# Decode attention with an MLP branch on one core: wo products, MLP pieces, value products and the last unit moved to other places in the order of work

## The chip, the core and the metric

The kernel runs on one NeuronCore of a Trainium2 chip. Its engines are TensorE (PE; PEld is its weight load), VectorE (DVE), ScalarE (ACT), GpSimd (POOL) and SyncE (SP), which here only issues transfers. Each engine works through its own instructions in order; semaphores order them against each other. The metric is the device time of one launch in microseconds (us). The time before is the median of three runs.

## What is computed

One decode step for 4 sequences: x is 4 x 640; layer normalisation gives xn. The result is x + A(xn) + B(xn).

```
A: q = xn @ wq                              # 32 heads of 128
   scores = q . k_cache * 128 ** -0.5       # 4 x 32 x 4096, no mask
   p = softmax(scores)
   o = p @ v_cache;  A = o @ wo             # wo: 4096 x 640
B: z = gelu(xn @ w_in)                      # tanh form; two halves of 864
   z2 = layernorm(z[864:])
   g = w_sp[0, 0] * z2 + b_sp[0]
   B = (z[:864] * g) @ w_out                # w_out: 864 x 640
```

All inputs are bf16. The K and V caches are 134 MB each; the profile counts 282.24 MB read from HBM in all. There is one query per head, so every element of K and V is used once.

## The kernel before

**Units and steps.** The work of attention is cut into 16 units: unit u = 4 hg + b is sequence b with the 8 heads of group hg (4 groups). A unit's K is 128 partitions x 256 rows of 128 numbers, 8.4 MB, and so is its V. A unit has 4 steps of 64 rows each; step n belongs to unit n // 4 and i = n % 4 is its place in it.

**A step.** VectorE multiplies a run of K by the broadcast q in place (`product`, L481) and adds its halves (`fold_half`, L487). TensorE adds the remaining 64 columns by 8 products with the identity (`sums`, L496). VectorE finishes the row sums (`row_sums`, L509), one step late, behind the next step's product. At the first step of a unit the unit before is finished: `head_max` (L518 to L525), `exps` on ScalarE (L531), `by_head` on VectorE (L542), which lays the weights out by head in `p_m` (two places, taken in turn).

**Value products.** `weighted` (L566) multiplies V by `p_m`, 64 products on TensorE; `take` (L578) copies the sum out on ScalarE. `turns` says behind which step of the next unit they stand: step 2 of it for units 0 to 11, step 3 for units 12 and 13. Unit 14's stand at the very end, behind the last exponentials and the denominators. At the first step of the unit after, `picked` gathers the rows of each head (L597; L644 in the last group).

**End of a group.** After the fourth unit of a group, `group_den` and `group_turn` give the group's denominators and the normalised, transposed heads (L607, L609, L617 on VectorE, at step 0 of a unit), and `group_proj` (L627) multiplies them with the group's wo rows, 16 products into `out_ps`, behind step 1's sums.

**Places and loads.** K lies in a ring of 7 places of one step each (`k_ring`); V has one place (`v_all`), which also holds wq, w_in and the end of w_out at the start. The rest of w_out lies in `p_m`. Odd units have ring places 0 to 3, even ones 3 to 6, and the last two units are placed apart; wo of a group lies in place 6, which the even units use too. All loads stand in one list, in order: the V of a unit, then the K of the unit two on, and so forth, with wo behind the K at the end of a group; the list's end interleaves halves of K with V, and unit 15's V goes to the ring in pieces. `pump` at the end of each step issues the loads of this list on SyncE until one needs a place that is still in use (`busy`); a place is given free where the program order has its last reader, and SyncE then waits for that reader by semaphore. So K of unit 6 and K of unit 10 come behind `group_proj`, and each V load behind the `weighted` of the unit before.

**The MLP.** `gmlp` (L347 to L454) is written behind the sums of step 1 as one block: 70 products `zT` (L355), the GELU (L362 to L375), sums for the norm (L380), the norm's factors on one partition (L389 to L416), their broadcast (L425), and 14 products into `out_ps` (L446). V's place is given free behind it.

**Order.** TensorE, VectorE, ScalarE and SyncE keep the order in which the program is written (`manual_schedule`); no planner moves anything.

Of the kernel before, what the change touches and what calls it, by code (L numbers as in the profile page):

```python
# [17 lines left out]
def kernel(  # L18
# [16 lines left out]
    Bsz, Sq, D = A_x.shape  # L35
# [16 lines left out]
    HG = H // HT  # L52
# [294 lines left out]
    def gmlp():  # L347
        zz, gw, gt, gz = (gm[n] for n in ("zz", "gw", "gt", "gz"))
        zT = ps_pv.tile([P, 2, NFC, Bsz], FP32, tag="pv", name="zT")
        for t in range(2):  # L350
            f1 = t * Fh + NFF * P
            w_t = w_in_sb[:, :, t * Fh : f1].rearrange("p c (f k) -> p c k f", k=NFF)
            for k in range(NFC):
                for c in range(DC):
                    nc.tensor.matmul(  # L355
                        out=zT[: P if k < NFF else FT, t, k, :],
                        lhsT=w_t[:, c, k, :] if k < NFF else w_in_sb[:, c, f1 : f1 + FT],
                        rhs=xnT[:, c, 0:Bsz],
                        start=(c == 0),
                        stop=(c == DC - 1),  # L360
                    )
        nc.vector.tensor_copy(out=zz[:, :, 0:NFF, :], in_=zT[:, :, 0:NFF, :])  # L362
        nc.vector.tensor_copy(out=zz[:FT, :, NFF, :], in_=zT[:FT, :, NFF, :])
        nc.vector.tensor_tensor(out=gw[:], in0=zz[:], in1=zz[:], op=ALU.mult)
        nc.vector.tensor_scalar(
            out=gw[:], in0=gw[:], scalar1=0.044715, scalar2=1.0, op0=ALU.mult, op1=ALU.add
        )
        nc.vector.tensor_tensor(out=gw[:], in0=gw[:], in1=zz[:], op=ALU.mult)
        nc.scalar.activation(
            out=gt[:], in_=gw[:], func=ACT.Tanh, scale=math.sqrt(2.0 / math.pi)  # L370
        )
        nc.vector.tensor_scalar(
            out=gt[:], in0=gt[:], scalar1=1.0, scalar2=0.5, op0=ALU.add, op1=ALU.mult
        )
        nc.vector.tensor_tensor(out=gz[:, 0:2], in0=zz[:], in1=gt[:], op=ALU.mult)  # L375
        sq = gz[:, 2, :, :]
        nc.vector.tensor_tensor(out=sq, in0=gz[:, 1, :, :], in1=gz[:, 1, :, :], op=ALU.mult)

        s_ps = ps_m.tile([1, 2, NFC, Bsz], FP32, tag="m", name="ln_ps")
        nc.tensor.matmul(  # L380
            out=s_ps[:], lhsT=ones_sq[:, 0:1], rhs=gz[:, 1:3], start=True, stop=True
        )
        st, ac = gm["st"], gm["ac"]
        mean_t = st[:, 0:Bsz]
        ex2_t = st[:, Bsz : 2 * Bsz]
        var_t = st[:, 2 * Bsz : 3 * Bsz]
        rst_t = st[:, 3 * Bsz : 4 * Bsz]
        tmp_t = st[:, 4 * Bsz : 5 * Bsz]
        nc.vector.tensor_reduce(  # L389
            out=st[:, 0 : 2 * Bsz].rearrange("o (s b) -> o s b", s=2),  # L390
            in_=s_ps[:].rearrange("o s k b -> o s b k"),
            axis=AX.X,
            op=ALU.add,
        )
        nc.vector.tensor_scalar(
            out=st[:, 0 : 2 * Bsz],
            in0=st[:, 0 : 2 * Bsz],
            scalar1=1.0 / float(Fh),
            scalar2=None,
            op0=ALU.mult,  # L400
        )
        nc.vector.tensor_tensor(out=tmp_t, in0=mean_t, in1=mean_t, op=ALU.mult)
        nc.vector.tensor_tensor(out=var_t, in0=ex2_t, in1=tmp_t, op=ALU.subtract)
        nc.scalar.activation(
            out=rst_t, in_=var_t, func=ACT.Sqrt, bias=eps_tile[:1], scale=1.0
        )
        wsp_t = work.tile([1, 1], FP32, name="wsp_t")
        nc.vector.tensor_copy(out=wsp_t[:], in_=wsp_bf[:])
        bsp_t = work.tile([1, 1], FP32, name="bsp_t")
        nc.vector.tensor_copy(out=bsp_t[:], in_=bsp_bf[:])  # L410
        nc.vector.reciprocal(out=rst_t, in_=rst_t)
        nc.vector.tensor_scalar(
            out=ac[:, 0:Bsz], in0=rst_t, scalar1=wsp_t[:, 0:1], scalar2=None, op0=ALU.mult
        )
        nc.vector.tensor_tensor(out=tmp_t, in0=ac[:, 0:Bsz], in1=mean_t, op=ALU.mult)
        nc.vector.tensor_scalar(  # L416
            out=ac[:, Bsz : 2 * Bsz],
            in0=tmp_t,
            scalar1=-1.0,
            scalar2=bsp_t[:, 0:1],  # L420
            op0=ALU.mult,
            op1=ALU.add,
        )
        ac_ps = ps_m.tile([P, 2 * Bsz], FP32, tag="m", name="ac_ps")
        nc.tensor.matmul(  # L425
            out=ac_ps[:], lhsT=ones_sq[0:1, :], rhs=ac[:], start=True, stop=True
        )
        ac_sb = work.tile([P, 2 * Bsz], FP32, name="ac_sb")
        nc.scalar.copy(out=ac_sb[:], in_=ac_ps[:])
        nc.vector.tensor_tensor(  # L430
            out=sq,
            in0=gz[:, 1, :, :],
            in1=ac_sb[:, None, 0:Bsz].to_broadcast([P, NFC, Bsz]),
            op=ALU.mult,
        )
        nc.vector.tensor_tensor(
            out=sq,
            in0=sq,
            in1=ac_sb[:, None, Bsz : 2 * Bsz].to_broadcast([P, NFC, Bsz]),
            op=ALU.add,  # L440
        )
        nc.vector.tensor_tensor(out=gm["yT"][:], in0=gz[:, 0, :, :], in1=sq, op=ALU.mult)
        for k in range(NFC):
            w = P if k < NFF else FT
            for half in range(2):
                nc.tensor.matmul(  # L446
                    out=out_sum(half),
                    lhsT=gm["yT"][:w, k, :],
                    rhs=(w_out_sb[:, k] if k < NFF else w_end_sb[:FT])[
                        :, half * NOH : (half + 1) * NOH  # L450
                    ],
                    start=False,
                    stop=False,
                )  # L454

    qbcs, scores, pvs = {}, {}, {}
    sums_ps, maxes, p_c = {}, {}, {}
# [21 lines left out]
    def product(n):  # L479
        u, r, t = step(n)  # L480
        nc.vector.tensor_tensor(  # L481
            out=t, in0=t, in1=qbcs[u][:, None, :].to_broadcast([P, HC, Dh]), op=ALU.mult
        )

    def fold_half(n):
        u, r, t = step(n)
        nc.vector.tensor_tensor(  # L487
            out=t[:, :, 0:HD2], in0=t[:, :, 0:HD2], in1=t[:, :, HD2:Dh], op=ALU.add
        )
# [134 lines left out]
    def group_proj(hg):  # L624
        for n, o in enumerate(gr.pop(hg)):
            for half in range(2):
                nc.tensor.matmul(  # L627
                    out=out_sum(half),
                    lhsT=o,
                    rhs=wo_sb[:, n, half * NOH : (half + 1) * NOH],  # L630
                    start=False,
                    stop=(hg == HG - 1 and n == HT - 1),
                )
        busy.remove(WO_AT)
# [18 lines left out]
        (pick_last if u // Bsz == HG - 1 else pick_unit)(u)  # L653


    turns = {NK * (u + 1) + 2: u for u in range(NU - 4)}
    turns[NK * (NU - 3) + 3] = NU - 4
    turns[NK * (NU - 2) + 3] = NU - 3

    E = mybir.EngineType  # L660
    with tc.manual_schedule(engines={E.PE, E.DVE, E.Activation, E.SP}):
        stage_q(0)
        waiting, closed = None, None
        for n in range(NK * NU):
            u, i = divmod(n, NK)
            product(n)
            if n:
                row_sums(n - 1)
            if i == 0 and u:
                head_max(u - 1)  # L670
                if waiting is not None:
                    picked(waiting)
                    if waiting % Bsz == Bsz - 1 and waiting // Bsz < HG - 1:
                        closed = waiting // Bsz
                    waiting = None
            fold_half(n)
            if i == 0 and u:
                exps(u - 1)
                by_head(u - 1)
            sums(n)  # L680
            if closed is not None:
                if i == 0:
                    group_turn(closed)
                else:
                    group_proj(closed)
                    closed = None
            if i == 0 and u + 1 < NU:
                stage_q(u + 1)
            if n == 1:
                gmlp()  # L690
                busy.remove(V)
            if n in turns:
                w = waiting = turns[n]
                if w % Bsz == Bsz - 1:
                    group_den(w // Bsz)
                weighted(w, v_runs)
                take(w)
                busy.remove(V)
            pump()
        row_sums(NK * NU - 1)  # L700
        head_max(NU - 1)
        exps(NU - 1)
# [8 lines left out]
        )  # L711
        rden = small.tile([P, NQ, PAR, Bsz], FP32, name="rden_all")
        nc.vector.reciprocal(out=rden[:], in_=den[:])
        weighted(NU - 2, v_runs)
        take(NU - 2)
        picked(NU - 2)
        u, b = NU - 1, Bsz - 1
        weighted(u, v_ends[0])
# [50 lines left out]
```

## Time and profile before

| what | us |
|---|---|
| median of three runs (679.65 to 680.65) | 680.4 |
| the profiled execution's own time | 679.59 |
| its span | 677.8 |
| VectorE busy | 522.5 |
| TensorE busy | 303.5 |
| L481 products busy (64) | 282.7 |
| L487 folds busy (64) | 145.9 |
| VectorE waiting for K | 98.1 |

The transfers moved 282.54 MB, 417 GB/s over the span; the queue of SyncE took 97.3% of the time of the 16 DMA engines. The mean granted clock of TensorE was 0.682 of its full speed.

How to read what follows: a group line has the source line, the engine, the operation, output and inputs with sizes, then the busy time, the mean of one in ns, and the idle time before it with what ended it. The page's slices divide the span by 40, some 16.9 us each. The chain of waits has start, length and what ended last; a DMA in it is the time from its issue to its landing. Times inside the execution are counted from the start of the span.

### The profile page before, as it was taken

Reading aid. Unit: us, or ns where it says so; the run is one execution under the profiler, and the core shown is the slowest. Engines: PE = TensorE matmul, PEld = TensorE weight load, DVE = VectorE, ACT = ScalarE, POOL = GpSimd, SP = SyncE. Lnnn points to the kernel's source line nnn. Section 1 sums busy time; section 2 is a strip of 40 time slices with the busy share of each in tenths; the row PEclk is TensorE's granted clock in tenths of the full one; section 3 lists DMA queues with packets and bytes.
Section 4 is the critical chain, followed back from the end, with each engine's and each line's share of the span. In section 5 each row is a group of like instructions: output and inputs, shape, how many; then the busy total and the mean of one; then the engine's idle time right before and its main releaser. Section 6 shows DMA issues by size and latency. Waiting matters only on the chain.

```text
span 677.8 us, 4614 instructions
## 1 busy us (share of the span) xinstructions
PE 303.5 (45%) x1999; PEld 128.0 (19%) x1999; DVE 522.5 (77%) x325; ACT 29.6 (4%) x73; POOL 2.7 (0%) x12
## 2 busy tenths in 40 slices
PE   0353472614546271452624546045462624636347
PEld 0131121211213020120211213012120211212114
DVE  2549989959696992968969696596969969997950
ACT  0010000000000000000000000000000000000000
POOL 1000000000000000000000000000000000000000
PEclk9755666767857676586766868558675766766678
DMA  9999999999999979999999989999999999999995
GB/s 374 438 438 433 434 419 418 430 433 433 434 433 379 465 321 433 430 433 429 426 426 437 403 375 372 433 433 434 433 434 433 433 437 430 401 451 428 436 405 204
DMA packets 8128, 282.54 MB, mean 417 GB/s; under 512 B 832, under 2 KB 1964, under 8 KB 3116
## 3 DMA queue, kind: packets, MB, share of 16 engines
q1 hardware_dynamic: 8088, 282.24, 97.3%
q8 instruction: 15, 0.25, 0.1%
q14 instruction: 5, 0.04, 0.0%
q10 hardware_dynamic: 20, 0.01, 0.0%
HBM read 282.24 MB, written 0.01 MB: 416 GB/s over the span
## 4 chain that ended last, share of the span: by engine, by line
DMA 54%; DVE 31%; PE 13%; issue 1%; ACT 1%; SPq 0%; DVEq 0%; ACTq 0%
DMA k_ring<-in_A_k_cache_dram 50%; DVE k_ring L481 16%; DVE k_ring L487 8%; PE s_ps L496 8%; DMA v_all<-in_A_v_cache_dram 5%; PE pv L566 2%; DVE s_sb L509 2%; DVE p_m L542 2%; DVE m L518 1%; PE out_ps L627 1%; PE zT L355 1%; PE o_last L722 0%; DVE mt L520 0%; DVE mt L523 0%; DVE nm L525 0%
## 5 line engine op out<-in xcount | busy, mean ns | idle before, releaser
L481 DVE TENSOR_TENSOR k_ring<-k_ring,qbc 128x8192 bf16<-128x8192 bf16 x64 | 282.7, 4417 | 98.1 <-DMA k_ring<-in_A_k_cache_dram 98.1
L496 PE MATMUL s_ps<-k_ring,ident 128*128 128x512 bf16 x512 | 199.9, 561 | 339.6 <-DVE k_ring L487 339.3
L496 PEld LDWEIGHTS <-ident 128*128 128x128 bf16 x512 | 65.9, 130 | 453.5 <-issue 379.5
L487 DVE TENSOR_TENSOR k_ring<-k_ring 128x4096 bf16<-128x4096 bf16 x64 | 145.9, 2280 | 0.0
L566 PE MATMUL pv<-v_all,p_m 128*32 128x512 bf16 x960 | 62.8, 421 | 2.4 <-DMA v_all<-in_A_v_cache_dram 2.4
L509 DVE TENSOR_REDUCE s_sb<-s_ps 128x64 f32<-128x512 f32 x64 | 43.6, 682 | 3.4 <-PE s_ps L496 3.4
L542 DVE TENSOR_TENSOR p_m<-p_c,own 128x2048 bf16<-128x2048 bf16 x16 | 36.6, 2286 | 5.2 <-ACT p_c L531 5.2
L566 PEld LDWEIGHTS <-p_m 128*32 128x32 bf16 x992 | 26.7, 105 | 41.4 <-issue 21.6
L578 ACT COPY o_rows<-pv 128x512 f32<-128x512 f32 x16 | 9.4, 586 | 314.2 <-PE pv L566 314.2
L531 ACT ACTIVATE p_c<-s_sb,nm 128x256 bf16<-128x256 f32 x16 | 8.1, 508 | 205.3 <-DVE nm L525 205.3
L597 PEld LDWEIGHTS o_ps<-o_rows,pick 128*128 128x128 f32 x96 | 12.6, 191 | 1.7
L597 PE MATMUL o_ps<-o_rows,pick 128*128 128x128 f32 x96 | 12.6, 275 | 0.0
L278 DVE TENSOR_SCALAR q_rows<-q_ps 128x512 bf16<-128x512 f32 x2 | 1.4, 692 | 13.7 <-PE q_ps L270 13.7
L730 DVE TENSOR_TENSOR o_n_last<-o_last,rden_all 128x32 bf16<-128x32 f32 x1 | 0.2, 193 | 14.3 <-PE o_last L722 14.3
L270 PE MATMUL q_ps<-v_all,xnT 128*32 128x512 bf16 x40 | 4.5, 630 | 10.4 <-DMA v_all<-in_A_wq_dram 10.4
L471 ACT CAST qbc<-qbc_ps 128x128 bf16<-128x128 f32 x16 | 4.3, 266 | 104.6 <-PE qbc_ps L463 104.6
L518 DVE TENSOR_REDUCE m<-s_sb 128x1 f32<-128x256 f32 x16 | 6.7, 420 | 0.6
L463 PE MATMUL qbc_ps<-q_rows,of_row 128*128 128x128 bf16 x32 | 6.4, 291 | 0.6 <-DVE q_rows L278 0.6
L463 PEld LDWEIGHTS <-of_row 128*128 128x128 bf16 x32 | 4.4, 139 | 8.5 <-issue 8.2
L362 DVE COPY zz<-zT 128x48 f32<-128x48 f32 x1 | 0.2, 207 | 7.2 <-PE zT L355 7.2
L644 PE MATMUL o_last<-hot,o_rows 128*128 128x8 f32 x32 | 4.2, 259 | 2.9 <-ACT o_rows L578 2.9
L644 PEld LDWEIGHTS o_last<-hot,o_rows 128*128 128x128 f32 x32 | 3.9, 191 | 4.9 <-ACT o_rows L578 4.9
(87 smaller groups left out, 71.3 us busy)
## 6 DMA issues: line engine op xcount, KB each, us to landing
k_ring<-in_A_k_cache_dram SPq DMA_DIRECT2D x6, 4096.0 KB, 20.6
v_all<-in_A_wq_dram SPq DMA_DIRECT2D x1, 5120.0 KB, 15.3
k_ring<-in_A_v_cache_dram SPq DMA_DIRECT2D x1, 4096.0 KB, 32.8
k_ring<-in_A_wo_dram SPq DMA_DIRECT2D x3, 1280.0 KB, 7.4
v_all<-in_B_w_in_dram SPq DMA_DIRECT2D x1, 2160.0 KB, 29.2
k_ring<-in_A_v_cache_dram SPq DMA_DIRECT2D x1, 2048.0 KB, 35.0
k_ring<-in_A_v_cache_dram SPq DMA_DIRECT2D x1, 1024.0 KB
k_ring<-in_A_v_cache_dram SPq DMA_DIRECT2D x2, 512.0 KB
```

The costliest lines, as they stand in the source:

```text
L463: nc.tensor.matmul(out=qb_ps[:], lhsT=of_row[:, e, b].rearrange("p k f l -> p (k f l)"), rhs=q_rows[e][:, hg, :], start=(e == 0), stop=(e ...
L481: nc.vector.tensor_tensor(out=t, in0=t, in1=qbcs[u][:, None, :].to_broadcast([P, HC, Dh]), op=ALU.mult)
L487: nc.vector.tensor_tensor(out=t[:, :, 0:HD2], in0=t[:, :, 0:HD2], in1=t[:, :, HD2:Dh], op=ALU.add)
L496: nc.tensor.matmul(out=s[:], lhsT=ident[:], rhs=t[:, :, g * RW : (g + 1) * RW], start=(g == 0), stop=(g == m - 1),)
L509: nc.vector.tensor_reduce(out=scores[u][:, r * HC : (r + 1) * HC], in_=sums_ps.pop(n)[:], axis=AX.X, op=ALU.add,)
L518: nc.vector.tensor_reduce(out=m1[:], in_=scores[u][:], axis=AX.X, op=ALU.max)
L531: nc.scalar.activation(out=p_c[u][:], in_=scores.pop(u)[:], func=ACT.Exp, bias=maxes.pop(u)[:], scale=1.0, accum_out=row_den[hg % NACC][:, ...
L542: nc.vector.tensor_tensor(out=p_m[:, u % 2], in0=p_c.pop(u)[:].rearrange("p (g c) -> p g c", c=CB)[:, :, :, None].to_broadcast([P, NG, CB, HT]
L566: nc.tensor.matmul(out=pvs[u][cg * QD : (cg + 1) * QD, :], lhsT=p_m[:, u % 2, g0 + n].rearrange("p c h -> p (c h)"), rhs=v_at[:, n * CB : ...
L578: nc.scalar.copy(out=o[:].rearrange("p c d -> p (c d)"), in_=pvs.pop(u)[:])
L597: nc.tensor.matmul(out=gr[hg][:], lhsT=pick[:, c, Bsz - 1 - b : P + Bsz - 1 - b], rhs=o[:, c, :], start=(b == 0 and c == 0), stop=(b == Bs ...
L644: nc.tensor.matmul(out=o_last[0][:, :, :, u % Bsz], lhsT=o[:, c, :], rhs=hot[:, c, :].rearrange("p (e k) -> p k e", e=PAR), start=(c == 0) ...
```

## The change

Four moves; no operation is added or left out.

1. `gmlp` becomes a generator of six pieces. The `zT` products stand behind step 0's sums and the next q broadcast. Behind step 1's product comes the GELU up to the tanh; behind step 1's fold come the rest of the GELU with the sums for the norm, and the norm's first factors; then step 1's sums. Behind step 2's product come the other factors and their broadcast, behind its fold the last piece with the 14 output products; then step 2's sums. V's place is given free behind step 2.
2. `turns` of units 0 to 11 say step 1, not step 2, of the next unit.
3. `group_turn` and `group_proj` stand together behind step 0's sums and the q broadcast of the unit after a group; before, the broadcast stood behind `group_turn`, and `group_proj` stood behind step 1's sums.
4. `weighted` and `take` of unit 14 stand ahead of the last `row_sums`, `head_max`, `exps` and `by_head`, directly behind the last sums.

```diff
@@ gmlp @@
                         stop=(c == DC - 1),
                     )
+        yield
         nc.vector.tensor_copy(out=zz[:, :, 0:NFF, :], in_=zT[:, :, 0:NFF, :])
...
             out=gt[:], in_=gw[:], func=ACT.Tanh, scale=math.sqrt(2.0 / math.pi)
         )
+        yield
...
             out=s_ps[:], lhsT=ones_sq[:, 0:1], rhs=gz[:, 1:3], start=True, stop=True
         )
+        yield
...
         nc.vector.tensor_copy(out=bsp_t[:], in_=bsp_bf[:])
+        yield
         nc.vector.reciprocal(out=rst_t, in_=rst_t)
...
         nc.scalar.copy(out=ac_sb[:], in_=ac_ps[:])
+        yield
...
                     stop=False,
                 )
+        yield
@@ the loop @@
-    turns = {NK * (u + 1) + 2: u for u in range(NU - 4)}
+    turns = {NK * (u + 1) + 1: u for u in range(NU - 4)}
...
         stage_q(0)
-        waiting, closed = None, None
+        waiting = None
+        mlp = gmlp()
         for n in range(NK * NU):
             u, i = divmod(n, NK)
             product(n)
+            if n in (1, 2):
+                next(mlp)
             if n:
                 row_sums(n - 1)
             if i == 0 and u:
                 head_max(u - 1)
                 if waiting is not None:
                     picked(waiting)
-                    if waiting % Bsz == Bsz - 1 and waiting // Bsz < HG - 1:
-                        closed = waiting // Bsz
-                    waiting = None
             fold_half(n)
+            if n == 1:
+                next(mlp)
+            if n in (1, 2):
+                next(mlp)
             if i == 0 and u:
                 exps(u - 1)
                 by_head(u - 1)
             sums(n)
-            if closed is not None:
-                if i == 0:
-                    group_turn(closed)
-                else:
-                    group_proj(closed)
-                    closed = None
             if i == 0 and u + 1 < NU:
                 stage_q(u + 1)
-            if n == 1:
-                gmlp()
+            if i == 0 and waiting is not None:
+                if waiting % Bsz == Bsz - 1:
+                    group_turn(waiting // Bsz)
+                    group_proj(waiting // Bsz)
+                waiting = None
+            if n == 0:
+                next(mlp)
+            if n == 2:
                 busy.remove(V)
             if n in turns:
                 w = waiting = turns[n]
...
             pump()
+        weighted(NU - 2, v_runs)
+        take(NU - 2)
         row_sums(NK * NU - 1)
         head_max(NU - 1)
         exps(NU - 1)
...
         nc.vector.reciprocal(out=rden[:], in_=den[:])
-        weighted(NU - 2, v_runs)
-        take(NU - 2)
         picked(NU - 2)
```

## The prediction, made before the changed kernel had run

> **What bounds the kernel now.** I read the page from the top: engine shares, the 40 slices, the chain that ended last.
>
> ```profile
> span 677.8 us, 4614 instructions
> PE 303.5 (45%) x1999; PEld 128.0 (19%) x1999; DVE 522.5 (77%) x325; ACT 29.6 (4%) x73; POOL 2.7 (0%) x12
> DMA  9999999999999979999999989999999999999995
> GB/s 374 438 438 433 434 419 418 430 433 433 434 433 379 465 321 433 430 433 429 426 426 437 403 375 372 433 433 434 433 434 433 433 437 430 401 451 428 436 405 204
> DMA 54%; DVE 31%; PE 13%; issue 1%; ACT 1%; SPq 0%; DVEq 0%; ACTq 0%
> L481 DVE TENSOR_TENSOR k_ring<-k_ring,qbc 128x8192 bf16<-128x8192 bf16 x64 | 282.7, 4417 | 98.1 <-DMA k_ring<-in_A_k_cache_dram 98.1
> ```
>
> No engine is full; the transfers are, at some 434 GB/s, and VectorE's 98.1 us of waiting is for K. So the time is what the transfer stream takes, plus its holes, plus the tail. The holes are the low slices: 14, then 22 to 24. The chain of waits, in order of time, says what makes the second:
>
> ```profile
> 395.66 0.31 DVE o_t L617
> ...
> 403.13 3.57 PE s_ps L496 x8
> 406.70 1.37 PE out_ps L627 x16
> 408.08 22.93 DMA k_ring<-in_A_k_cache_dram
> ```
>
> The transposed group is ready at 395.97, but its wo products (L627) stand behind the next step's sums, and K of unit 10 needs the wo place. SyncE's timeline and the windows (second column: us; the last two: DMA share, GB/s) show an empty queue:
>
> ```profile
> 380.71 0.38 SPq L202 DMA_DIRECT2D k_ring<-in_A_wo_dram  x1
> 381.14 0.46 SPq L147 DMA_DIRECT2D v_all<-in_A_v_cache_dram  x1
> 408.08 0.33 SPq L138 DMA_DIRECT2D k_ring<-in_A_k_cache_dram  x1
> 417.40 0.33 SPq L147 DMA_DIRECT2D v_all<-in_A_v_cache_dram  x1
> ```
> ```profile
> 240.80:245.20 4.40, 3.55 (x22) 1.30 (x21) 4.40 (x3) 0.00 (x0) 0.00 (x0) 0.73 0.00 0
> 404.80:408.90 4.10, 3.25 (x21) 1.20 (x20) 4.10 (x3) 0.00 (x0) 0.00 (x0) 0.73 0.00 0
> ```
>
> The V load of unit 8 (381.14), asked alone, answers
>
> ```profile
> DMA to landing us min/median/max: 26.2/26.2/26.2
> ```
>
> so it landed at 407.3; K was issued only at 408.08. Both group ends have over 4 us with nothing moving.
>
> **Size of the holes.** The step-0 product of a unit starts when its K lands. In the chain these stand at 103.01, 143.18, 181.87, 220.53, 266.30, 306.60, 345.49, 384.09, 431.11, 469.83, 508.86, 547.32. Undisturbed units take 38.68 (143.18 to 181.87 to 220.53). From 220.53 to 384.09 are four units and a wo load: 163.6 - 4 x 38.68 - 3.0 = 5.9 over. (wo's 3.0: the third, issued at 542.91, landed at 550.28, K of unit 13 ahead of it at 547.3.) From 384.09 to 547.32: 5.5 over. At the head K of unit 1 landed at 63.1 (issued 36.21, 26.9 later): to 103.0 is 39.9, 1.2 over; to 143.18 another 40.17, 1.5 over.
>
> **wo products behind the transposes.** Nothing is added; 16 products (1.23 to 1.71 us) move from behind the sums of step 37 to behind those of step 36 and the q broadcast, which end near 396.3; o_t is ready at 395.97, wo landed about 388. So K of unit 10 goes out near 397.9, not 408.08, and that of unit 6 near 234.2, not 244.38: before V's end at 404.8 and 240.8, by 6 us or more. The moved wait (PE for o_t) has only step 37's sums behind it, whose fold ends at 403.1; SyncE's next is V of the following unit; GpSimd issues nothing here. The third group's products move too, to no use: K of unit 14 does not need the wo place.
>
> **Value products a step sooner.** In a unit landing at L, sums of step 1 end at L + 22.7 at a group end (384.0 to 406.7) and about L + 21.3 elsewhere; V lands at L + 23.3 (407.3) and L + 19.3 (unit 7: issued 338.64, 26.0 later, K of unit 8 at 345.4). So PE waits 0.6 us at worst, and 64 value products (3.8 to 4.5) end before the next fold or near it; row sums come 4.3 us later still: free. The V issue moves ahead some 7 us behind a K already queued (V of unit 9 was issued 13.6 us before K of unit 10 landed): it fills the head's 1.5 hole. One cost: today value products in step 2 leave PE warm for step 3's sums (215.05, 1.90 us); a step sooner these start at 213.95, with the fold, after 5 us of idling, at 3.57: they end 0.55 later, and wo's load waits for them. The first two wo loads were issued 3.5 and 3.3 us ahead of K's landing and lost about 1.0 to 1.1 (V of unit 8: 407.3 against 384.0 + 3.0 + 19.3 = 406.3); the third, 4.3 ahead, lost none. So I price lead below 4.4 at its own length: after, 1.65, 1.65 and 0.5. **Groups: (5.9 - 1.65) + (5.5 - 1.65) - 0.5 = 7.6**; if that loss vanishes 11.4; if each wo load loses 1.1 more and the third 0.5 is kept, 5.4.
>
> **MLP in pieces.** The same instructions; before, VectorE did nothing else from 39.6 to 53.0, 7.2 of it waiting for zT. Now zT's 70 products (3.72) follow the first sums and broadcast: 36.4 to 40.1; VectorE, done with product 1 at 36.9, waits 3.2 for them; then 1.1 (to the tanh), row sums 0.6, fold 2.2, the norm's first half with its product 2.0: step 2's product starts at 46.0, not 53.0. Then 4.4, second half 0.9, 0.6, fold 2.2, last piece 0.65: 54.75. The 14 output products (1.94) now stand ahead of step 2's sums, which end near 60.4, and VectorE waits 1.3 for them behind its next product: step 4 starts at 63.3 instead of 67.28, just as K of unit 1 lands (63.1). V of unit 0 goes out at 56.9, 1.8 later, with 6 us of K still queued: no cost. If that cover were gone it would be 1.8. K of unit 2 goes out 4.0 sooner, which removes the 1.2; V of unit 1 near 88 rather than 99.65, the 1.5. **Head: 2.7**, at least 0.
>
> **Unit 14 ahead of the last sums.** The timeline of PE (start, us, ..., idle before) and two windows (third column from the end: the granted clock):
>
> ```profile
> 584.13 3.79 PE L566 MATMUL pv<-v_all,p_m 128*32 128x512 bf16 x64
> 649.04 3.30 PE L496 MATMUL s_ps<-k_ring,ident 128*128 128x512 bf16 x8 [3.56 <-DVE k_ring L487]
> 657.39 0.63 PE L705 MATMUL den_all<-acc,ones_sq 128*128 128x32 f32 x2 [5.05 <-DVE acc L551]
> 657.95 6.11 PE L566 MATMUL pv<-v_all,p_m 128*32 128x512 bf16 x64
> ```
> ```profile
> 652.40:657.40 5.00, 0.01 (x1) 0.01 (x1) 4.07 (x7) 0.60 (x2) 0.00 (x0) 0.84 0.95 410
> 657.40:664.10 6.70, 6.66 (x66) 2.66 (x66) 0.36 (x1) 0.00 (x0) 0.00 (x0) 0.58 0.98 412
> ```
>
> Right behind sums, 64 value products took 3.79; after 5 us of idling, 6.11. So 652.36 + 3.79 = 656.15. The copy of unit 14 is now ahead of the last exponentials on ScalarE: these start 0.49 after it (as at 624.17 and 624.66), at 656.7 instead of 654.31, and everything to the denominators 2.4 later: 659.8, then 0.56 to 660.35. Behind that stand unit 14's 8 picks and unit 15's 32 products, which ended at 667.68: at full clock 1.06 + 1.91, at half 2.12 + 3.06 (half of 6.11), so they end at 663.3 or 665.5. A clock of 0.84 over the 5 us idle window means a drop 3.4 after the last sum; the new idle stretch, 656.15 to 659.8, is 3.65, and 0.58 over 6.7 us means 5.6 at half. So half: **tail 2.1**. Ends: the last wo piece was issued at 662.62 and landed 8.5 later, 671.1; two more products (0.26) give 671.35 against 675.03, so 3.7 at most. If value products take 6.11 even behind the sums, -0.2.
>
> The Trainium skill (TensorE: Matmul & The Clock Gate, Seeing it yourself) shows one run that re-throttled only 5.2 us after its last matmul; by that figure PE would still be at full clock. That row of this trace says 3.4, so I keep 2.1. By that figure rival (a) follows.
>
> **Sum.** 7.6 + 2.7 + 2.1 = 12.4 off the profiled execution's 679.6 (span 677.8, 1.8 around it): 667.2. The median of the runs shown is 0.8 above that execution, so 668.0.
>
> **Rivals.** (a) PE keeps full clock through the last idle stretch: tail 3.7, 666.4; for it, 3.65 is hardly past 3.4. (b) The head or the tail gives nothing, because K of unit 1 is late anyway or the exponentials behind the copy eat all: 670.7 or 670.1. (c) The hole stays: K of units 6 and 10 held by something else that ends as late. Then 2.7 + 2.1 - 1.6 (wo later): 677.2. Against it: each ready time above is 6 us clear. (d) Slower: outstanding loads share the engines instead of queueing, so V issued 7 us sooner pushes K back. K's next issue follows its landing by 12 and then misses the end of V at 19.3 once K slips over 7; at a 13.5 slip some 6 us lie empty in each of 11 units, 66 - 12 gives 734; it ends slower from about 8.2. Against it: V of unit 9, 13.6 us ahead of K's landing, left K at 22.9 from issue to landing, V of unit 5 at 21.8. (e) The sooner steps change nothing because some other wait replaces them: 680.4.
>
> **Numbers.** Forecast 0.50, (a) 0.22, (b) 0.14, (c) 0.07, (d) 0.04, (e) 0.03. Low end: 11.4 + 2.7 + 3.7 = 17.8, 662.6; high end of the unknown costs: 5.4 + 0 - 0.2, 675.2. I say 663.0 to 673.5, which leaves out the extremes together. A change under 0.2% (1.4 us) cannot be told from none: faster 0.93 (forecast, a, b, c), within 0.03, slower 0.04.
>
> **What would show it.** K of units 6 and 10 issued near L + 14 and no empty window in front; unit starts 38.7 apart, 42 to 43.5 over a wo load; step 4 starting near 63; value products of unit 14 right behind the last sums in about 3.8, exponentials behind their copy. It is wrong if the empty windows stand elsewhere (in front of the wo or V loads), if K lands later after its issue than 22 plus what is queued, or if the end waits for the last wo piece.

## The result

The changed kernel takes 671.3 us (median of six runs, 667.9 to 675.2) against 680.5 for the kernel before. The ratio is 0.986, with a 95% interval of 0.982 to 0.990: some 9.5 us off. The forecast was 668.0, range 663.0 to 673.5. Its profiled execution took 668.8, with a span of 667.0 instead of 677.8. Single executions of these kernels and of the kernel before took 695 to 731 us; no median, ratio or timeline here uses them.

The page of the changed kernel, the lines that answer to those shown before:

```profile
span 667.0 us, 4615 instructions
DMA  9999999999999999999999999999999999999995
GB/s 376 421 465 436 425 429 421 433 440 440 429 436 402 451 432 432 437 436 436 433 429 422 409 424 441 436 437 436 436 437 436 405 436 398 415 459 436 401 414 221
DMA 61%; DVE 25%; PE 12%; issue 1%; ACT 0%; SPq 0%; DVEq 0%; ACTq 0%
L487 DVE TENSOR_TENSOR k_ring<-k_ring,qbc 128x8192 bf16<-128x8192 bf16 x64 | 282.8, 4419 | 91.6 <-DMA k_ring<-in_A_k_cache_dram 91.6
```

(The products of L481 are now at L487, the sums at L502, the wo products at L633, the value products at L572.) VectorE's work did not change by a microsecond. The low slices 14 and 22 to 24 (counted from 0) are gone: where there were 321 and then 403, 375 and 372 GB/s stand 432 and then 409, 424 and 441. At the two group ends the chain of waits (start, length, what ended last) now reads:

```profile
229.91 0.32 DVE o_t L623
230.24 0.04 issue
230.28 1.27 PE out_ps L633 x16
231.57 28.70 DMA k_ring<-in_A_k_cache_dram
...
389.35 1.63 PE out_ps L633 x16
391.00 29.29 DMA k_ring<-in_A_k_cache_dram
```

K of unit 6 is issued right behind the wo products, 13 us sooner than before, while V of unit 4 is still on its way; of its 28.7 us to landing some 19 are its own part of the stream (half of the 38.6 us from unit to unit), the rest is time in the queue. Around these two places the windows (second column: us; last two: DMA share, GB/s) show a full stream where there had been over 4 us without a byte:

```profile
228.00:244.00 16.00, 9.65 (x88) 4.09 (x90) 15.86 (x10) 0.27 (x1) 0.00 (x0) 0.84 1.01 435
386.00:402.00 16.00, 9.52 (x54) 3.54 (x56) 15.86 (x10) 0.27 (x1) 0.00 (x0) 0.66 1.00 434
```

Where the 10.8 us of the two profiled executions came from, by the start of each unit's first product: unit 3 starts 2.1 sooner (141.08 against 143.18), unit 13 11.0 sooner (536.31 against 547.32), V of unit 13 lands 10.2 sooner (608.66 against 618.87), and the span ends 10.8 sooner. So: head 2.1, group ends 8.1, end 0.6.

The end is the surprise. TensorE's timeline in the changed kernel (start, us, ..., idle before), then a window over it (third column from the end: granted clock):

```profile
638.95 3.20 PE L502 MATMUL s_ps<-k_ring,ident 128*128 128x512 bf16 x8 [3.56 <-DVE k_ring L493]
642.08 3.96 PE L572 MATMUL pv<-v_all,p_m 128*32 128x512 bf16 x64
649.71 0.63 PE L717 MATMUL den_all<-acc,ones_sq 128*128 128x32 f32 x2 [3.68 <-DVE acc L557]
650.16 1.85 PE L650 MATMUL o_last<-hot,o_rows 128*128 128x8 f32 x8
651.94 3.60 PE L572 MATMUL pv<-k_ring,p_m 128*32 128x512 bf16 x32
656.29 1.88 PE L650 MATMUL o_last<-hot,o_rows 128*128 128x8 f32 x8 [0.75 <-ACT o_rows L584]
658.02 3.56 PE L732 MATMUL o_last<-p_m,k_ring 128*128 128x8 bf16 x128
661.87 2.30 PE L633 MATMUL out_ps<-k_ring,o_n_last 128*4 128x320 bf16 x16 [0.28 <-DVE o_n_last L740]
```
```profile
649.70:664.20 14.50, 13.42 (x194) 9.38 (x194) 0.55 (x2) 0.59 (x1) 0.00 (x0) 0.50 0.68 272
```

Unit 14's products run in 3.96 behind the sums, as forecast. But then TensorE idles for 3.68 us, and from there to the end the clock stays at half, although TensorE is busy for 13.42 of 14.50 us. Before, the last picks and the products behind them had run after the clock had come up again:

```profile
668.40 1.06 PE L644 MATMUL o_last<-hot,o_rows 128*128 128x8 f32 x8 [0.75 <-ACT o_rows L578]
669.32 3.35 PE L722 MATMUL o_last<-p_m,k_ring 128*128 128x8 bf16 x128
672.96 2.06 PE L627 MATMUL out_ps<-k_ring,o_n_last 128*4 128x320 bf16 x16 [0.28 <-DVE o_n_last L730]
```

From the end of the last sums to the copy of the result it takes 22.06 us (642.15 to 664.21); before, 22.71 (652.34 to 675.05).

### The profile page after: what moved, and what is told of

It reads as the page before. It is cut to its first block, busy times and chain, and to the rows that moved or that the text cites. A ratio compares the mean times of both kernels' runs of the same rounds, so it can differ in the third digit from the quotient of the medians.

```text
span 667.0 us, 4615 instructions
## 1 busy us (share of the span) xinstructions
PE 310.5 (47%) x1999; PEld 136.1 (20%) x1999; DVE 522.5 (78%) x325; ACT 29.5 (4%) x73; POOL 2.7 (0%) x12
## 4 chain that ended last, share of the span: by engine, by line
DMA 61%; DVE 25%; PE 12%; issue 1%; ACT 0%; SPq 0%; DVEq 0%; ACTq 0%
DMA k_ring<-in_A_k_cache_dram 56%; DVE k_ring L487 13%; PE s_ps L502 7%; DVE k_ring L493 7%; DMA v_all<-in_A_v_cache_dram 5%; PE pv L572 3%; DVE s_sb L515 2%; DVE p_m L548 1%; DVE m L524 1%; PE out_ps L633 1%; PE o_last L650 1%; PE o_last L732 1%; DVE mt L526 0%; DVE mt L529 0%; DVE nm L531 0%
## 5 line engine op out<-in xcount | busy, mean ns | idle before, releaser
L487 DVE TENSOR_TENSOR k_ring<-k_ring,qbc 128x8192 bf16<-128x8192 bf16 x64 | 282.8, 4419 | 91.6 <-DMA k_ring<-in_A_k_cache_dram 91.6
L502 PE MATMUL s_ps<-k_ring,ident 128*128 128x512 bf16 x512 | 199.9, 561 | 316.4 <-DVE k_ring L493 316.3
L502 PEld LDWEIGHTS <-ident 128*128 128x128 bf16 x512 | 65.3, 130 | 429.7 <-issue 381.5
L572 PE MATMUL pv<-v_all,p_m 128*32 128x512 bf16 x960 | 60.5, 409 | 4.7 <-DMA v_all<-in_A_v_cache_dram 4.7
L515 DVE TENSOR_REDUCE s_sb<-s_ps 128x64 f32<-128x512 f32 x64 | 43.8, 684 | 4.2 <-PE s_ps L502 4.2
L572 PEld LDWEIGHTS <-p_m 128*32 128x32 bf16 x992 | 26.6, 104 | 42.8 <-issue 19.7
L603 PEld LDWEIGHTS o_ps<-o_rows,pick 128*128 128x128 f32 x96 | 19.4, 280 | 4.1 <-issue 3.0
L603 PE MATMUL o_ps<-o_rows,pick 128*128 128x128 f32 x96 | 18.3, 355 | 0.0
L650 PE MATMUL o_last<-hot,o_rows 128*128 128x8 f32 x32 | 5.8, 310 | 2.2 <-ACT o_rows L584 2.2
L650 PEld LDWEIGHTS o_last<-hot,o_rows 128*128 128x128 f32 x32 | 5.5, 261 | 4.1 <-ACT o_rows L584 4.1
L633 PE MATMUL out_ps<-k_ring,o_t 128*4 128x320 bf16 x48 | 5.2, 378 | 0.1
## 6 DMA issues: line engine op xcount, KB each, us to landing
k_ring<-in_A_k_cache_dram SPq DMA_DIRECT2D x6, 4096.0 KB, 20.1
```

The source lines that it names most:

```text
L487: nc.vector.tensor_tensor(out=t, in0=t, in1=qbcs[u][:, None, :].to_broadcast([P, HC, Dh]), op=ALU.mult)
L502: nc.tensor.matmul(out=s[:], lhsT=ident[:], rhs=t[:, :, g * RW : (g + 1) * RW], start=(g == 0), stop=(g == m - 1),)
L515: nc.vector.tensor_reduce(out=scores[u][:, r * HC : (r + 1) * HC], in_=sums_ps.pop(n)[:], axis=AX.X, op=ALU.add,)
L572: nc.tensor.matmul(out=pvs[u][cg * QD : (cg + 1) * QD, :], lhsT=p_m[:, u % 2, g0 + n].rearrange("p c h -> p (c h)"), rhs=v_at[:, n * CB : ...
L603: nc.tensor.matmul(out=gr[hg][:], lhsT=pick[:, c, Bsz - 1 - b : P + Bsz - 1 - b], rhs=o[:, c, :], start=(b == 0 and c == 0), stop=(b == Bs ...
L633: nc.tensor.matmul(out=out_sum(half), lhsT=o, rhs=wo_sb[:, n, half * NOH : (half + 1) * NOH], start=False, stop=(hg == HG - 1 and n == HT ...
```

## Experiments

Theory H: the time is the transfer stream, and most of the gain is the two holes at the group ends, which the place of the wo products closes alone. Rival S: the queue is kept full because V goes out a step sooner. For the end: theory A, the order on ScalarE (exponentials behind the copy) is what held the gain back; theory C, the half clock is; rival B, the half clock comes whatever stands before.

| kernel | ratio to before | interval | units over a wo load apart, us | last sums to result, us |
|---|---|---|---|---|
| before | 1 | | 45.8, 47.0 | 22.7 |
| changed | 0.986 | 0.982 to 0.990 | 42.0, 43.2 | 22.1 |
| wo products alone | 0.989 | 0.984 to 0.993 | 41.7, 43.2 | 21.8 |
| all but the wo products | 0.998 | 0.994 to 1.001 | 46.5, 47.2 | 22.2 |
| all but the sooner step | 0.983 | 0.977 to 0.988 | 42.2, 42.6 | 20.8 |
| copy behind exponentials | 0.981 | 0.976 to 0.986 | 42.9, 43.6 | 18.3 |
| MLP in one block | 0.986 | 0.983 to 0.990 | 43.8, 42.7 | 20.8 |
| group's last unit in step 2 | 0.983 | 0.981 to 0.986 | 41.7, 42.6 | 22.2 |
| idle stretch filled | 0.983 | 0.980 to 0.985 | 43.8, 43.3 | 20.1 |

The last two columns are read off the timelines of each kernel's one profiled execution; "units over a wo load" is the time between the first products of two units with a wo load between their K, at the first two group ends.

### The wo products alone, and all but them

```diff
# on the kernel before
+            if i == 0 and u + 1 < NU:
+                stage_q(u + 1)
             if closed is not None:
-                if i == 0:
-                    group_turn(closed)
-                else:
-                    group_proj(closed)
-                    closed = None
-            if i == 0 and u + 1 < NU:
-                stage_q(u + 1)
+                group_turn(closed)
+                group_proj(closed)
+                closed = None
```

> Only the wo products move (behind the transposes); MLP, value products and the end stand as before. Theory H (the time is the transfer stream, and the two holes at the group ends are most of the gain): both holes of 4.4 and 4.1 us close, units over a wo load start 42.8 us apart instead of 45.8 and 47.0, about 9 us off, near 671.5. Rival S (the queue is fed because V is issued a step sooner): the holes move in front of the V loads and under 3 us come off, 678 or more.

Measured: 674.1 us, ratio 0.989: 7.8 off, interval 4.5 to 11.2. Both holes closed (41.7 and 43.2). Its profiled execution ran its first loads slowly (see the last section), so its head cannot be compared.

The other way round, the changed kernel with `group_proj` behind step 1's sums again:

> The changed kernel with the wo products back behind step 1's sums. H: both holes are back, only the head (2.2) and the end (0.6 to 2) stay: 677 to 679. S: the V issue a step sooner keeps the queue full, so it stays near the changed kernel, 670 to 673.

Measured: 679.4 us, ratio 0.998, the interval reaching 1.001. The holes are back, though V goes out in step 1. SyncE's timeline and two windows of this kernel:

```profile
379.50 0.46 SPq L147 DMA_DIRECT2D v_all<-in_A_v_cache_dram  x1
406.65 0.33 SPq L138 DMA_DIRECT2D k_ring<-in_A_k_cache_dram  x1
410.12 0.33 SPq L147 DMA_DIRECT2D v_all<-in_A_v_cache_dram  x1
```
```profile
240.40:243.40 3.00, 2.53 (x22) 0.92 (x24) 3.00 (x3) 0.00 (x0) 0.00 (x0) 0.72 0.05 22
404.20:407.20 3.00, 3.00 (x38) 1.42 (x40) 3.00 (x3) 0.00 (x0) 0.00 (x0) 0.72 0.00 0
```

K of unit 10 goes out at 406.65, and V behind it in the list cannot pass it. The two halves add up: 7.8 and 1.6 against the 9.5 of the whole, though each has an interval of 2 to 3 us to either side; the holes, there in one kernel and gone in the other, decide. H holds, S falls.

### Value products in step 2 again, and only at a group's end

```diff
-    turns = {NK * (u + 1) + 1: u for u in range(NU - 4)}
+    turns = {NK * (u + 1) + 2: u for u in range(NU - 4)}
```

> The changed kernel with the value products back in step 2. H: no hole at the group ends (42.6 us over a wo load); the sums ahead of the wo load are warm again (1.9 instead of 3.6 us), so that load goes out some 0.5 us sooner three times; V of unit 1 goes out 7 us later and loses what it gained at the head, at most 1.5. Together within 1 us of the changed kernel. S: holes of some us in front of V loads, 3 us or more above the changed kernel.

Measured: 669.0 us, ratio 0.983, with unit starts at 140.8 (unit 3) and 534.8 (unit 13) against 141.1 and 536.3. No hole in front of V, and nothing lost at the head: V of unit 1 went out at 95.6, 6.6 us ahead of K of unit 2. So a step sooner earned nothing that shows: the ratio is 0.003 below the changed kernel's, and the intervals overlap. The next kernel takes it back for units 3, 7 and 11 alone:

```diff
-    turns = {NK * (u + 1) + 1: u for u in range(NU - 4)}
+    turns = {
+        NK * (u + 1) + (2 if u % Bsz == Bsz - 1 else 1): u for u in range(NU - 4)
+    }
```

> The changed kernel with the value products of a group's last unit alone back in step 2, so that the sums ahead of the wo load run right behind them. If the slow sums cost the wo load its lead: those sums take 1.9 us instead of 3.6, units over a wo load start 0.4 us closer, about 1 us off in all. If not: no change.

Measured: ratio 0.983, units over a wo load 41.7 and 42.6 apart. The sums in front of the first wo load, TensorE and SyncE, in the changed kernel and then in this one:

```profile
211.86 2.79 PE L502 MATMUL s_ps<-k_ring,ident 128*128 128x512 bf16 x8 [4.54 <-DVE k_ring L493]
214.68 0.38 SPq L202 DMA_DIRECT2D k_ring<-in_A_wo_dram  x1
218.34 4.43 DVE L487 TENSOR_TENSOR k_ring<-k_ring,qbc 128x8192 bf16<-128x8192 bf16 x1 [6.53 <-DMA k_ring<-in_A_k_cache_dram]
```
```profile
208.10 3.65 PE L572 MATMUL pv<-v_all,p_m 128*32 128x512 bf16 x64
211.69 1.90 PE L502 MATMUL s_ps<-k_ring,ident 128*128 128x512 bf16 x8
213.62 0.38 SPq L202 DMA_DIRECT2D k_ring<-in_A_wo_dram  x1
218.19 4.42 DVE L487 TENSOR_TENSOR k_ring<-k_ring,qbc 128x8192 bf16<-128x8192 bf16 x1 [6.55 <-DMA k_ring<-in_A_k_cache_dram]
```

Behind the value products the sums take 1.90, after idling 2.79, and the wo load gets a lead of 4.6 us over K's landing instead of 3.7. Over all profiles without the old holes, group ends with the last unit's value products in step 2 (four executions, two ends each) lie 42.4 apart in the mean, those in step 1 (seven executions) 43.3: 0.9 us per group end for the sooner step. Between the executions' totals this is within the spread; the unit starts show it. The lead of the wo load differs by 0.8 in the mean (4.0 against 3.3), but from one group end to the next a longer lead does not always go with a shorter distance (a lead of 3.85 with 43.9, one of 2.85 with 42.7), so that the lost lead is the cause is argued, not shown.

### The MLP in one block again

```diff
-            if n == 0:
-                next(mlp)
-            if n == 2:
+            if n == 1:
+                for _ in mlp:
+                    pass
                 busy.remove(V)
# and the calls of next(mlp) behind the products and folds of steps 1 and 2 taken out
```

> The changed kernel with the MLP as one block behind step 1's sums again. Theory H: step 4 starts near 67.3 instead of 63.8, K of unit 2 goes out near 79.3 instead of 75.8 and lands 0.5 to 1.2 us later; V of unit 1, still a step sooner, goes out near 92.5, 10 us ahead of that landing, so no hole before K of unit 3. All later starts 0.5 to 1.2 us later, 1 us above the changed kernel. Rival M (the pieces carry the head's whole gain): 2.2 us above it.

Measured: 670.4 us, ratio 0.986, as the changed kernel. Unit 1 starts at 66.9 instead of 63.8, but unit 2 at 102.3 (changed: 102.5) and unit 3 at 140.9 (141.1): no later at all. The chain of waits says why; K of unit 2 goes out 3 us later and is that much shorter in the queue:

```profile
78.96 23.21 DMA k_ring<-in_A_k_cache_dram
114.10 26.70 DMA k_ring<-in_A_k_cache_dram
```

in the changed kernel:

```profile
75.84 26.55 DMA k_ring<-in_A_k_cache_dram
114.19 26.80 DMA k_ring<-in_A_k_cache_dram
```

V of unit 0 was still being moved in both. So at the head there was one hole, in front of V of unit 1 (99.65 before, 3.4 ahead of K's landing), and either edit closes it: the pieces with V at 95.6, the sooner step with V at 92.7. Neither is missed while the other stands.

### The end: copy behind the exponentials

```diff
         weighted(NU - 2, v_runs)
-        take(NU - 2)
         row_sums(NK * NU - 1)
         head_max(NU - 1)
         exps(NU - 1)
+        take(NU - 2)
         by_head(NU - 1)
```

> The changed kernel with the copy of unit 14 behind the last exponentials on ScalarE. Theory A (the order on ScalarE is what kept the end from gaining): exponentials 2.4 us sooner, TensorE idles only 1.2 us before the denominators and keeps full clock, and the end waits for the last wo piece: from the landing of V of unit 13 to the end of the span 56.5 us instead of 58.3, about 1.8 off the changed kernel. Rival B (the half clock does it, whatever the order): picks and products of the end again at half clock, under 0.7 off.

Measured: 667.6 us, ratio 0.981. TensorE's timeline:

```profile
643.80 4.20 PE L572 MATMUL pv<-v_all,p_m 128*32 128x512 bf16 x64
648.93 0.41 PE L717 MATMUL den_all<-acc,ones_sq 128*128 128x32 f32 x2 [0.94 <-DVE acc L557]
649.18 1.04 PE L650 MATMUL o_last<-hot,o_rows 128*128 128x8 f32 x8
650.15 1.91 PE L572 MATMUL pv<-k_ring,p_m 128*32 128x512 bf16 x32
658.01 0.60 PE L732 MATMUL o_last<-p_m,k_ring 128*128 128x8 bf16 x16 [0.64 <-DMA k_ring<-in_A_v_cache_dram]
...
660.13 2.01 PE L633 MATMUL out_ps<-k_ring,o_n_last 128*4 128x320 bf16 x12 [0.53 <-DMA k_ring<-in_A_wo_dram]
```

The window from the denominators to the second picks (third column from the end: granted clock):

```profile
648.93:653.86 4.93, 4.18 (x56) 3.02 (x57) 0.36 (x1) 0.59 (x1) 0.00 (x0) 1.00 0.98 415
```

The exponentials no longer wait, the idle stretch shrinks to 0.94 us, the clock holds through the picks and unit 15's products (it falls to half in the 128 x 8 products behind them, between 655 and 656), and now the last products wait for pieces of V and of wo: 18.3 us from the last sums to the result, bound by the landing of the last wo piece. This kernel changes both the wait and the clock, so the next one changes the clock alone.

### The end: the idle stretch filled

```diff
         take(NU - 2)
+        idle = ps_s.tile([P, HC, RW], FP32, name="s_ps")
+        for _ in range(16):
+            nc.tensor.matmul(
+                out=idle[:].rearrange("p c w -> p (c w)"),
+                lhsT=ident[:],
+                rhs=q_rows[0][:].rearrange("p g d -> p (g d)"),
+                start=True,
+                stop=True,
+            )
         row_sums(NK * NU - 1)
```

> The changed kernel with 16 more products (128 x 512, into a place that nobody reads) on TensorE between unit 14's value products and the denominators; the exponentials stay behind the copy. Theory C (the idle stretch of 3.7 us drops the clock, and the half clock costs the end its gain): picks 1.06 instead of 1.85, products 1.91 instead of 3.60, second picks 1.06 instead of 1.88; from the end of the last sums to the copy of the result 18.5 to 19.5 us instead of 22.06, 2.5 to 3.5 off the changed kernel, then the last wo piece bounds it. Rival B (half clock whatever TensorE does before): unchanged, or later by what the extra products delay the denominators.

Measured: 669.1 us, ratio 0.983.

```profile
648.54 3.40 PE L714 MATMUL s_ps<-q_rows,ident 128*128 128x512 bf16 x15 [0.16 <-issue]
652.30 1.04 PE L650 MATMUL o_last<-hot,o_rows 128*128 128x8 f32 x8
653.27 1.91 PE L572 MATMUL pv<-k_ring,p_m 128*32 128x512 bf16 x32
655.92 1.06 PE L650 MATMUL o_last<-hot,o_rows 128*128 128x8 f32 x8 [0.75 <-ACT o_rows L584]
660.68 0.60 PE L741 MATMUL o_last<-p_m,k_ring 128*128 128x8 bf16 x16 [0.78 <-DMA k_ring<-in_A_v_cache_dram]
```
```profile
652.05:656.98 4.93, 4.18 (x56) 3.01 (x57) 0.36 (x1) 0.59 (x1) 0.00 (x0) 1.00 0.96 394
```

The denominators come as late as before (7.7 us after the last sums against 7.6), the granted clock is 1.00 through the second picks, and the picks take 1.04 and 1.06 instead of 1.85 and 1.88, the products 1.91 instead of 3.60: 3.3 us. Of these 1.9 reach the result (20.1 us from the last sums instead of 22.1; I had expected 18.5 to 19.5), because the last V piece and the wo pieces are waited for. For the picks and unit 15's products C holds and B falls; behind 659 the clock is at half here too, in the 128 x 8 products. A is true as well, since taking away the wait shortens the idle stretch too. In the executions' times the gain is not shown: 0.983 against 0.986, with overlapping intervals.

### All on one chip, and a faster kernel

The copy behind the exponentials and the value products in step 2 together ("copy behind, step 2") were run twice, first beside the filled idle stretch:

> The changed kernel with the copy of unit 14 behind the last exponentials and the value products in step 2 again: wo order, MLP pieces and unit 14's products are what is left of the change. Theory H with A: units over a wo load 42.2 to 42.8 apart, the end as in the run with the copy behind the exponentials (18.3 us from the last sums to the copy of the result): 1 us or less below that run, 666 to 667.5. Theory S: above it by 2 or more.

Measured: 667.0 us, ratio 0.980 (0.977 to 0.983); no timeline of it is used. Then four kernels on one chip, kernel before at 680.0:

> The changed kernel once more, beside the next three on one chip. From its first profile: 668.8 to 671.3; the holes at the group ends stay closed, and TensorE's clock at the end is at half or goes up early, by chance, which moves the end by up to 1.3 us.

> The changed kernel with unit 14's value products and their copy back behind the denominators. Theory C (half clock eats what the move gains): 0.6 us slower than the changed kernel, from the end of the last sums to the copy of the result 22.7 us. My forecast's own term: 2.1 slower.

> Again the copy of unit 14 behind the last exponentials, value products in step 1: 666.7 to 668, 2 to 3.5 below the changed kernel of the same chip; end 18.3 us from the last sums, bound by the last wo piece.

> The same with the value products in step 2; its first profile was of a disturbed execution. If a step sooner is worth anything, this is above the run before it; theory H has it within 1 us of it, below rather than above (666 to 667.5), with 42.2 to 42.8 over a wo load.

| kernel | median us | ratio | interval | units over a wo load | last sums to result |
|---|---|---|---|---|---|
| changed | 672.6 | 0.988 | 0.985 to 0.991 | 43.1, 43.9 | 22.0 |
| end undone | 671.8 | 0.988 | 0.986 to 0.991 | 43.8, 43.2 | 23.4 |
| copy behind exponentials | 667.4 | 0.982 | 0.979 to 0.984 | 43.8, 43.4 | 20.8 |
| copy behind, step 2 | 666.0 | 0.979 | 0.977 to 0.982 | 42.4, 42.5 | 19.3 |

The move of unit 14's products by itself is worth nothing that the times show; in the profiles it is worth 1.4 here. Over all timelines the end takes 21.8 to 23.4 us with the old order (three of them) and 20.8 to 22.2 with the new one (six): 0.9 in the mean. With the copy behind the exponentials the move is worth some 4 in the times. But the 18.3 us at the end, expected again for that kernel, came as 20.8: the idle stretch was 1.44 us this time, the clock fell to half some 1.9 us behind it (0.93 over 650 to 651, 0.50 from there), and the last wo piece was waited for. The changed kernel itself, at 672.6, came out above the 668.8 to 671.3 expected for it. The last kernel is faster than both the kernel before and the changed one. That its step 2 is better than step 1 fits the 0.9 us per group end, but the intervals of these two overlap, so the times alone do not show it.

## Why the prediction was right, and where it was off

**What bounds the kernel.** Right: no engine's work changed, and the gain is transfer time without a byte that is gone.

**wo products (7.6 of the sum, group ends).** Right, in place and size. K of unit 6 was forecast for 234.2 less what the head gained; it came at 231.57. The forecast had 43.3 us from unit to unit over a wo load; they came 42.0 and 43.2. The group ends gave 8.9 up to unit 13 (3.7 and 3.8 over the two wo loads, 1.7 in the unit behind the first, 0.3 lost elsewhere), where 8.1 was forecast; 0.8 of it went again by the landing of V of unit 13, behind the third wo load, where 0.5 was priced. That leaves 8.1 against 7.6. The rivals (c), the hole stays, and (d), loads share the engines, are out: undisturbed units stayed 38.6 to 38.8 apart, but for one at 39.4, with V issued 13 us or more ahead of K's landing.

**The warm sums.** The forecast's one cost of the sooner step, 0.55 us of lead lost by the wo load, was real and somewhat small: 0.9 us per group end. The forecast let the sooner step fill the hole at the head in exchange. This was the error: without the sooner step unit 3 starts no later (140.8 against 141.1), since the pieces close that hole alone.

**Head (2.7).** The size was nearly right (2.1), the times too (step 4 forecast for 63.3, came at 63.82; K of unit 2 for 75.2, came at 75.84). The working was wrong in one step: I gave 1.2 us to K of unit 2 going out 4 us sooner and 1.5 to V of unit 1. The 1.5 came (unit 2 to unit 3: 40.17 before, 38.60 after); it is one hole, and either of two edits closes it. Of the 1.2 only 0.5 came (unit 2 at 102.48 instead of 103.01), and not from the sooner issue: the block kernel shows K of unit 2 landing no later when it goes out at 78.96. What the 0.5 comes from stays open.

**End (2.1).** This step failed in its size: 0.6 in the profiles, and nothing in the times. The wait behind the copy (forecast 2.4, measured 2.5), the drop of the clock in a 3.7 us idle stretch and the half clock for the picks and products were as forecast (the picks took 1.85 where 2.12 was priced, the products 3.60 where 3.06 was: the 6.11 that I halved had run partly at full clock); these ended 13.4 us after the last sums instead of 15.3, so 1.9 had been gained by then. Then I priced everything behind them at its old durations, taking the clock to be up again after 5.6 us. It stayed at half, and the second picks (1.88 against 1.06), the products with V (3.56 against 3.35) and the last wo products (2.30 against 2.06) gave 1.3 back. In two later timelines of the same order the clock was up again at the second picks, and the end took 20.8 us instead of 22.06, so part of this size is chance.

The one run that I weighed there (the Trainium skill, TensorE: Matmul & The Clock Gate, Seeing it yourself: a re-throttle 5.2 us after the last matmul) would by its figure have kept the clock up and made rival (a). This trace differs from that run: an idle stretch of 3.68 us was enough here, and one of 0.94 us was not. The measurement decides. The same page's table (What's actually happening) has the clock come up after about 3.4 us of sustained work; over the 14.5 us in which TensorE was 93% busy here it did not.

**The sum.** 12.4 was forecast and 10.8 came in the profiled executions, which makes 667.2 and 668.8. The median is 2.5 above the changed kernel's profiled execution, where I had added 0.8. So 9.3 came off the median, not 12.4: 671.3 lies inside the range, but nearer to rival (b), where the end gives nothing (670.1), than to the 668.0 of the forecast.

## What to carry to other kernels

In a kernel bound by its transfers, look for windows without a byte and ask which instruction frees the place that the next load waits for; moving that last reader forward is worth the whole window, and issuing other loads sooner is worth nothing if they stand behind it in the same list. When two edits feed the same empty stretch, count it once, and price a sooner issue at nothing where the queue ahead of it is still full. And when work is moved out of an idle stretch, ask what the idle time that is left does to the clock of everything behind it, to the very end.

## What I had not expected of the hardware

**The clock at the end.** TensorE at half clock for 14.5 us while busy for 13.42 of them; the products there are short (128 x 8 in three of the six groups). In the kernels "all but the sooner step" and "MLP in one block" the same order had its second picks back at 1.06 us, so it is not the same every time. The clock also falls without such an idle stretch: in the kernel with the idle stretch filled TensorE is busy throughout 657 to 659 with 128 x 8 products, and the granted clock goes from 1.00 to 0.50 by 659 to 660; in the kernel before it was 1.00 up to 673 and 0.62 from there to 674, behind the same products. What holds the clock or brings it up in such work stays open.

**Slow loads at the start.** The changed kernel's second profiled execution took 675.4 us, 6.6 more than its first. Windows of the first, then of the second (last column GB/s):

```profile
42.00:62.00 20.00, 9.37 (x34) 3.31 (x35) 18.23 (x23) 2.55 (x4) 0.00 (x0) 0.66 1.06 459
62.00:82.00 20.00, 7.71 (x20) 2.66 (x20) 18.62 (x13) 0.87 (x3) 0.00 (x0) 0.68 0.98 423
```
```profile
42.00:62.00 20.00, 9.41 (x34) 3.32 (x35) 18.18 (x23) 2.23 (x4) 0.00 (x0) 0.66 1.07 413
62.00:82.00 20.00, 7.30 (x18) 2.47 (x18) 15.33 (x11) 0.87 (x3) 0.00 (x0) 0.66 0.94 374
```

The DMA engines are as busy and move some 11% less; unit 2 starts at 106.8 instead of 102.5, and that 4.3 us is never made up, since nothing after it has slack. "wo products alone" had the same start (397 GB/s between 62 and 82, unit 2 at 107.2). It accounts for two thirds of the difference between these two executions. What makes the loads slow in some executions was not tried.
